# The first part of an attention and expert kernel in another order, with products of zeros on TensorE and the softmax guard on VectorE

## Chip, cores, metric

One core of one Trainium2 chip runs the whole program. The metric is the device time of one execution in microseconds (us). The engines are TensorE (PE; its weight loads are PEld), VectorE (DVE), ScalarE (ACT), GpSimd (POOL), and SyncE (SP), whose queue issues nearly all transfers. Each engine takes its instructions strictly in the order of its own row.

## The reference, cut to what matters

Three layers follow each other: sparse attention, a two-matrix layer with a PReLU, and a mixture of four experts.

```python
# attention, 2 batches x 8 heads x 768 tokens x 64: a local window and 24 block summaries
scores_l = scale * np.matmul(q, k.transpose(0, 1, 3, 2))           # kept where |i - j| < 16
scores_s = scale * np.einsum('bhsd,bhnd->bhsn', q, k_sum) + np.log(block)
a = np.exp(scores_all - np.max(scores_all, axis=-1, keepdims=True))
a = a / (np.sum(a, axis=-1, keepdims=True) + 1e-09)                # 1e-09: the guard
x = np.matmul(a, v_all)                                            # -> 1536 tokens x 512
# layer 2: 512 -> 2048 -> 512
h = x @ w_in
x = (np.maximum(h, 0.0) + alpha * np.minimum(h, 0.0)) @ w_out
# layer 3: four experts, 512 -> 1024 -> 512 each
for e in range(E):
    out += p[:, e:e + 1] * (np.maximum(x @ w1[e], 0.0) @ w2[e])
```

## The kernel before, in words

Every product that needs full precision is made of three: each operand is split into a high and a low part (h and l in the names), and high by high, high by low and low by high are added up in PSUM.

The program has a first part, ordered by hand, and a second one, which a scheduler orders. The first part holds the whole attention, a quarter of layer 2 (the first four of sixteen blocks of the inner dimension) and the preparation of the first sixteen weight pieces. The second part holds the rest of layer 2 and the experts.

The attention runs over 24 half tiles (128 tokens by four heads). A half tile goes through these steps, each with its two letters in the order: load of keys (`fa`), queries (`fb`) and values (`fc`); scores on TensorE (`sa`, line 219); masked maximum on VectorE (`sb`, line 229, eight instructions); exponentials with their row sums on ScalarE (`sc`, line 238); the guard, which adds 1e-9 to the four sums (`na`, line 245, on GpSimd); its reciprocal on VectorE (`nb`, line 248); the scaling on ScalarE (`nc`, line 257); four transposes on TensorE (`ta`, line 263); their copy on ScalarE (`tb`); the value product (`xa`, line 281); and its split into high and low (`xb` on ScalarE, `xc` on VectorE, line 298). `ka`, `kb`, `kc` load and reduce the block maxima of the keys, `va` to `vf` the block sums of the values.

A weight piece comes as 64-bit numbers, and VectorE and ScalarE turn it into two 32-bit ones: `wa` loads it, `wb` to `wh` and `wj` are seven instructions of VectorE but for `wc` (ScalarE), `wi` is the high part on ScalarE. Pieces 0 to 3 and 4 to 7 are those of `w_in` and `w_out` that the first quarter of layer 2 needs. `la` to `le` are the first product of layer 2 for 256 tokens and one piece, with its PReLU and its split; `ma` and `mb` are the second product and its copy. `pa` is the first product of the second part, drawn ahead.

`ORDER` is one string of such steps, played once from left to right: each step appends its instructions to the rows of its engines and its transfers to SP's queue. A step that has to wait holds back everything behind it on its engine, and nothing on the others. A transfer also waits for the one that used its completion lane before it.

Of the kernel before, what the change touches and what calls it, by code (L numbers as in the profile page):

```python
# [8 lines left out]
F32 = mybir.dt.float32  # L9
# [3 lines left out]
ALU = mybir.AluOpType  # L13
# [4 lines left out]
P = 128  # L18
# [15 lines left out]
G = 4  # L34
# [6 lines left out]
CH = 512  # L41
# [7 lines left out]


ORDER = (
# [34 lines left out]
)  # L86
MASK_OFF = -1.0e9 * math.sqrt(D)
EXP_LOW = float((1023 - 127 + 20) << 20)
# [4 lines left out]
def kernel(  # L93
# [15 lines left out]
    nc = tc.nc  # L109
# [4 lines left out]
    ps_2 = ctx.enter_context(tc.tile_pool(name="ps_2", bufs=3, space=PSUM))  # L114
# [4 lines left out]
    att1 = first.enter_context(tc.tile_pool(name="att1", bufs=1))  # L119
# [13 lines left out]

    ident = att1.tile([P, P], F32, name="ident")
    mask = att1.tile([P, 3, NK], F32, name="mask")
    ksum = att1.tile([P, HP, 1, NB], F32, name="ksum")

    kwb = [[att1.tile([P, NK // NB, 2, 2, NB], F32, name=f"kw{hh}{i}") for i in range(3)] for hh in range(2)]
# [3 lines left out]
    st = {"kv": 0}  # L142
# [11 lines left out]
    def half_tile(i):  # L154
        b, r = divmod(i, 2 * NAC)
        return b, r // 2, r % 2
# [51 lines left out]
    def load_vw(i):  # L208
        b, ac, hh = half_tile(i)
        st["vc", b, ac] = t = v_free.pop(0)  # L210
        nc.sync.dma_start(out=t[0:KW], in_=vw_in[b, ac])

    def a_scores(i):
        b, ac, hh = half_tile(i)
        q, kw = st.pop(("q", i)), st.pop(("kw", i))
        kw_free[hh].append(kw)
        st["s", i] = sp = ps_s.tile([P, 4, NK], F32, tag="s", name="s")
        for u in range(4):
            nc.tensor.matmul(sp[:, u], q[:, u // 2, u % 2], kw[:, :, u // 2, u % 2], start=True, stop=True)  # L219
# [22 lines left out]

    def a_guard(i):
        st["r", i] = r = att.tile([P, 4], F32, tag="r", name="r", bufs=3)
        nc.gpsimd.tensor_scalar(r, st.pop(("e", i)), 1e-9, None, op0=ALU.add)

    def a_recip(i):
        nc.vector.reciprocal(st["r", i], st["r", i])
# [290 lines left out]
    def split3(ps, terms):  # L539
        n = len(terms)  # L540
        for i, (a, c) in enumerate(terms):
            ins = nc.tensor.matmul(ps, a, c, start=(i == 0), stop=(i == n - 1))  # L542
        return ins

    def l1_product(i, c0, n):
        wh, wl = ws[0, i]
        c = slice(c0, c0 + n)
        ps = ps_1.tile([P, n], F32, tag="l1", name="l1")
        terms = []
        for k in range(KD):  # L550
            kk = slice(k * P, (k + 1) * P)
            terms += [(wh[:, kk], xh[:, k, c]), (wh[:, kk], xl[:, k, c]), (wl[:, kk], xh[:, k, c])]
        split3(ps, terms)
        gs[i, c0] = [ps]
# [288 lines left out]
    def l2_steps(u):  # L843
        n, c0, size = units[u]
        return [lambda d=d: l2a(n, d, c0, size) for d in range(KD)]
# [12 lines left out]
    load_q(2, nc.scalar)  # L858
    nc.scalar.dma_start(out=mask, in_=mask_in)
    nc.scalar.dma_start(out=ident, in_=ident_in)  # L860
    nc.gpsimd.memset(ebias, -EXP_LOW)
    nc.gpsimd.memset(vs, 0.0)
    nc.scalar.activation(early, ebias, AF.Exp)
# [6 lines left out]
    def column(f):  # L870
        return lambda u, d, *on: f(0, d, u * C0, C0, *on)

    stage = {
        "pa": lambda: l1_product(G, 0, CH),
        "ka": k_load, "kb": k_max, "kc": k_copy,
        "va": v_load, "vb": v_sum, "vc": v_rows,
        "vd": lambda b: v_mean(b, 0), "ve": lambda b: v_mean(b, 1), "vf": v_copy,
# [9 lines left out]
    with tc.manual_schedule():  # L887
        for x in ORDER.split():
            a, on = (x[2:-1], x[-1:]) if x[-1] in "vg" else (x[2:], "")
            ins = stage[x[:2]](*((int(a),) if x[0] in "fsntxw" else [int(c) for c in a]), *on)  # L890
            if x[:2] in ("ma", "wa", "le"):
                final[x[:2]] = ins
    for ins in final.values():
# [49 lines left out]
    with tc.manual_schedule(engines={mybir.EngineType.PE, mybir.EngineType.Activation}):  # L943
        left, keep, carry = [], [], []
        l2 = l2_steps(len(units) - 1)[KD // 2:]
# [7 lines left out]
        def standard(s, l2, left):  # L953
            p1, p2, p6, p5, p7, p4, p3 = e_steps(s)
            if s > NQ and not left:
                left, l2 = l2[:2], l2[2:]
            if s == NQ - 1:
                for k in range(2):
                    own_sums(k, False)
            for f in [p1] + left[:1] + [p2] + carry[:1] + [p6] + carry[1:2] + left[1:] + [p5] + carry[2:] + [p7]:  # L960
                f()
            side = e_prep(s + 1)
            carry[:] = []
            if s + 1 < NQ and (s + 1) % 2 == 0:
                side, carry[:] = side[:-3], side[-3:]
            if s in own_at:
                side = side[:3] + own_at[s] + side[3:]
            keep = l2[-1:] if s == 2 * NQ - 1 else []
            merge(l2[:len(l2) - len(keep)], side)
            return [lambda i=i, s=s: l2b(s, i) for i in range(NAC)], [p4, p3], keep  # L970
# [24 lines left out]
        for s in range(UA):  # L995
            l2, left, _ = standard(s, l2, left)
# [3 lines left out]
        for a in range(UA, UB, 2):  # L1000
# [7 lines left out]
            else:  # L1008
                n = 13 - done
# [10 lines left out]
        l2, left = [lambda i=i: l2b(UB, i) for i in range(NAC)], []  # L1020
        for s in range(UB + 1, 2 * NQ):
            l2, left, keep = standard(s, l2, left)
# [62 lines left out]
```

## Time and profile before

| | us |
|---|---|
| median of 3 runs | 833.74 |
| lowest, highest | 833.1, 835.07 |
| the profiled execution, as timed | 835.03 |
| its span, first to last instruction | 833.2 |

The profiled execution is the upper end of the three. Its span leaves out 1.83 us of its own time. The profile says of each engine when it was busy and what ended its waits. Since TensorE is busy for 98% of the span, the few places where it waits or runs at half its clock are what an edit can win; all other engines matter only where TensorE waits for them.

### The profile page before, as it was taken

How to read it: one execution, taken by the hardware profiler on the slowest of the kernel's cores; microseconds unless marked ns; L12 is line 12 of the kernel's file. 1: busy time of each engine (PE TensorE's matmuls, PEld its weight loads, DVE VectorE, ACT ScalarE, POOL GpSimd, SP SyncE). 2: the span in 40 equal slices, each digit the busy share in tenths (PEclk: the TensorE clock that was granted, in tenths of full speed). 3: DMA queues.
4: the chain of work that ended last, by engine and by line, in shares of the span. 5: the costliest groups of instructions: out<-in, count | busy, mean ns of one | idle time of the engine just before them, and what ended most of it. 6: DMA issues, size and time to landing. Idle time of an engine off the chain costs nothing.

```text
span 833.2 us, 14458 instructions
## 1 busy us (share of the span) xinstructions
PE 814.2 (98%) x5000; PEld 746.2 (90%) x5000; DVE 612.6 (74%) x1284; ACT 424.9 (51%) x1048; POOL 307.5 (37%) x302
## 2 busy tenths in 40 slices
PE   4899999999999999999999999999999999999998
PEld 3689999888888888988989989989999999999997
DVE  7998667999993446587687687687677677768765
ACT  5999995543442333353454454464455454455430
POOL 1110100000013100386886886789153354354330
PEclk9799999999999999999999999999999999999999
DMA  9999413333222100367867867869766856767622
GB/s 340 298 276 303 145 45 102 102 101 101 95 84 76 51 1 0 102 205 263 284 214 267 282 212 271 276 233 324 263 226 202 266 187 220 246 209 238 201 72 76
DMA packets 97496, 155.37 MB, mean 186 GB/s; under 512 B 9872, under 2 KB 48272, under 8 KB 97424
## 3 DMA queue, kind: packets, MB, share of 16 engines
q1 hardware_dynamic: 96704, 153.92, 56.8%
q8 instruction: 39, 0.64, 0.3%
q10 hardware_dynamic: 720, 0.55, 0.2%
q14 instruction: 33, 0.27, 0.1%
HBM read 106.71 MB, written 47.71 MB: 185 GB/s over the span
## 4 chain that ended last, share of the span: by engine, by line
PE 91%; DMA 3%; DVE 3%; ACT 2%; issue 0%; SPq 0%; POOL 0%; ACTq 0%
PE l L542 48%; PE cb L662 16%; PE l2q L784 13%; PE cd L662 8%; PE ca L662 4%; PE s L219 1%; PE xps L281 1%; DMA kw<-in_kw 1%; DMA vcat<-in_vw 1%; PE pt L263 1%; DMA acc<-in_kt 1%; ACT sm L238 1%; DMA bl<-dt 0%; DVE xel L617 0%; DVE sm L229 0%; DVE ksum L169 0%
## 5 line engine op out<-in xcount | busy, mean ns | idle before, releaser
L391 POOL TENSOR_TENSOR w0l<-ra,w0h 128x256 fp32r<-128x256 f32 (+1 forms) x32 | 37.6, 1176 | 237.1 <-ACT w0h L390 237.1
L831 DVE SCALAR_TENSOR_TENSOR acc<-l,prob_sb,acc 128x512 f32<-128x512 f32 x101 | 74.2, 746 | 26.0 <-PE l L542 25.8
L795 DVE SCALAR_TENSOR_TENSOR acc<-l2q,prob_sb,acc 128x256 f32<-128x256 f32 x156 | 71.2, 478 | 27.3 <-PE l2q L784 25.4
L542 PE MATMUL l<-xh,w0h 128*128 128x512 f32 (+1 forms) x240 | 84.5, 352 | 0.0
L542 PE MATMUL l<-gh,w1h 128*128 128x512 f32 (+1 forms) x240 | 83.3, 350 | 0.0
L542 PE MATMUL l<-xl,w0h 128*128 128x512 f32 (+1 forms) x240 | 83.1, 346 | 0.0
L542 PE MATMUL l<-xh,w0l 128*128 128x512 f32 (+1 forms) x240 | 83.1, 346 | 0.0
L542 PE MATMUL l<-gh,w1l 128*128 128x512 f32 (+1 forms) x240 | 83.0, 347 | 0.0
L542 PE MATMUL l<-gl,w1h 128*128 128x512 f32 (+1 forms) x240 | 81.4, 347 | 0.0
L542 PE MATMUL l<-w1h,gl 128*128 128x512 f32 x192 | 75.0, 391 | 0.0
L542 PE MATMUL l<-w1l,gh 128*128 128x512 f32 x192 | 75.0, 391 | 0.0
L542 PE MATMUL l<-w1h,gh 128*128 128x512 f32 x192 | 74.7, 389 | 0.0
L567 DVE SCALAR_TENSOR_TENSOR l<-m,beta,l 128x512 f32<-128x512 f32 (+1 forms) x60 | 38.6, 644 | 23.8 <-ACT m L561 23.7
L685 ACT ACTIVATE u<-cb 128x384 f32<-128x384 f32 x64 | 31.3, 489 | 47.5 <-PE cb L662 47.5
L561 ACT ACTIVATE m<-l 128x512 f32<-128x512 f32 (+1 forms) x60 | 30.6, 513 | 48.2 <-PE l L542 48.1
L542 PEld LDWEIGHTS l<-xh,w0h 128*128 128x128 f32 x240 | 45.4, 189 | 5.9
L542 PEld LDWEIGHTS l<-gh,w1h 128*128 128x128 f32 x240 | 45.4, 189 | 5.7
L542 PEld LDWEIGHTS l<-gh,w1l 128*128 128x128 f32 x240 | 45.4, 189 | 5.6
L542 PEld LDWEIGHTS l<-xl,w0h 128*128 128x128 f32 x240 | 45.4, 189 | 5.6
L542 PEld LDWEIGHTS l<-gl,w1h 128*128 128x128 f32 x240 | 45.4, 189 | 5.5
L542 PEld LDWEIGHTS l<-xh,w0l 128*128 128x128 f32 x240 | 45.3, 189 | 5.6
L391 POOL TENSOR_TENSOR w1l<-rb,w1h 128x512 fp32r<-128x512 f32 x32 | 43.9, 1391 | 11.9 <-ACT w1h L390 11.9
(167 smaller groups left out, 2534.3 us busy)
## 6 DMA issues: line engine op xcount, KB each, us to landing
raw<-in_wa SPq DMA_DIRECT2D x32, 512.0 KB, 3.9
rb<-in_wb SPq DMA_DIRECT2D x16, 512.0 KB, 4.8
ra<-in_wb SPq DMA_DIRECT2D x32, 256.0 KB, 3.6
dt<-xh SPq DMA_DIRECT2D x28, 256.0 KB, 2.4
dt<-xl SPq DMA_DIRECT2D x28, 256.0 KB, 3.3
bh<-dt SPq DMA_DIRECT2D x28, 256.0 KB, 3.7
bl<-dt SPq DMA_DIRECT2D x28, 256.0 KB, 3.7
q<-in_qh SPq DMA_DIRECT2D x23, 256.0 KB, 5.8
```

The costliest lines, as they stand in the source:

```text
L219: nc.tensor.matmul(sp[:, u], q[:, u // 2, u % 2], kw[:, :, u // 2, u % 2], start=True, stop=True)
L238: nc.scalar.activation(sm[:, u], sm[:, u], AF.Exp, bias=mx[:, u:u + 1], scale=-1.0, accum_out=sume[:, u:u + 1],)
L263: nc.tensor.transpose(pt[0:NK, u], pp[:, u], ident)
L391: nc.gpsimd.tensor_tensor(lo, src, hi.bitcast(F32), op=ALU.subtract)
L542: ins = nc.tensor.matmul(ps, a, c, start=(i == 0), stop=(i == n - 1))
L561: nc.scalar.activation(m, gs[i, c0][0], AF.Relu, scale=-1.0)
L567: nc.vector.scalar_tensor_tensor(ps, m, beta[:, i:i + 1], ps, op0=ALU.mult, op1=ALU.add)
L662: nc.tensor.matmul(ps, l, r, start=(first and i == 0), stop=(i == len(terms) - 1), skip_group_check=True)
L685: nc.scalar.activation(v[name], ps, AF.Copy)
L784: nc.tensor.matmul(ps, l, r, start=(first and j == 0), stop=(j == len(terms) - 1), skip_group_check=True)
L795: nc.vector.scalar_tensor_tensor(dst, ps, pe, dst, op0=ALU.mult, op1=ALU.add)
L831: added = nc.vector.scalar_tensor_tensor(acc2[:, t], ps, pe, acc2[:, t], op0=ALU.mult, op1=ALU.add)
```

## The change

Three edits, all in the first part. `ORDER` is a new string: the same steps, in another sequence. A new step `zz` followed by a number n issues n products of a 128 x 128 tile of zeros with itself into a PSUM tile that nobody reads; nine such steps, 39 products in all, stand among the first TensorE steps, the last just ahead of the first value product. The guard `na` moves from GpSimd to VectorE. A clearing of the tile of zeros is added on GpSimd. Of the order only the first line stands here.

```diff
 ORDER = (
-    "wa5 wd5 wb5 we5 ka01 wc5 kb01 ka00 fa2 kb00 kc00 sa2 wf5 wa3 wg5 fa0 wh5 wb3 wd3 fb0 wi5 ka03 sa0 "
...
+    "wa5 wd5 ka01 wb5 wc5 we5 ka00 kb01 wf5 wa3 kb00 wg5 kc00 wd3 fa2 wh5 wi5 wb3 fa0 we3 fb0 wj5 wa2 "
+    "zz15 sa2 zz1 wc3 fb4 fa4 sb2 ka02 wf3 wb2 sa0 zz5 sc2 na2 wd2 wc2 sb0 sc0 wg3 fb1 nb2 sa4 zz2 na0 "
...
+    zero = att1.tile([P, P], F32, name="zero")
...
+    zps = ps_2.tile([P, P], F32, tag="l2", name="zps")
+
+    def spin(n):
+        for _ in range(n):
+            nc.tensor.matmul(zps, zero, zero, start=True, stop=True)
...
     def a_guard(i):
         st["r", i] = r = att.tile([P, 4], F32, tag="r", name="r", bufs=3)
-        nc.gpsimd.tensor_scalar(r, st.pop(("e", i)), 1e-9, None, op0=ALU.add)
+        nc.vector.tensor_scalar(r, st.pop(("e", i)), 1e-9, None, op0=ALU.add)
...
+    nc.gpsimd.memset(zero, 0.0)
...
-        "pa": lambda: l1_product(G, 0, CH),
+        "zz": spin, "pa": lambda: l1_product(G, 0, CH),
```

On TensorE, at the start of the program, stood scores (`s`), transposes (`pt`) and nothing else:

```order
L219 MATMUL s<-kw_97,q 128x120 x4
L219 MATMUL s<-kw_98,q 128x120 x4
L219 MATMUL s<-kw_99,q 128x120 x4
L263 MATMUL pt<-ident,sm 120x128 x4
L219 MATMUL s<-kw_100,q 128x120 x4
```

On TensorE, at the same place, `zps` is the tile that the products of zeros write:

```order
L218 MATMUL zps<-zero 128x128 x15
L226 MATMUL s<-kw_98,q 128x120 x4
L218 MATMUL zps<-zero 128x128
L226 MATMUL s<-kw_99,q 128x120 x4
L218 MATMUL zps<-zero 128x128 x5
L226 MATMUL s<-kw_100,q 128x120 x4
L218 MATMUL zps<-zero 128x128 x2
L270 MATMUL pt<-ident,sm 120x128 x4
```

Each group of zeros stands ahead of a step that TensorE reached early before.

On VectorE, ahead of the first masked maximum (`ISA sm,mx`), stood two block maxima together and the preparation of one and a bit weight pieces:

```order
L169 TENSOR_REDUCE ksum<-acc 128x24 x2
L174 COPY kw_97<-ksum 128x96
L338 TENSOR_SCALAR e<-e 128x512
L342 SCALAR_TENSOR_TENSOR e<-raw,e 128x512
L348 TENSOR_TENSOR t<-t,e 128x512
L314 TENSOR_SCALAR e<-raw 128x512
L327 TENSOR_SCALAR t<-raw 128x512
L229 ISA sm,mx<-s,mask 128x120
```

On VectorE, at the same place, now:

```order
L170 TENSOR_REDUCE ksum<-acc 128x24
L345 TENSOR_SCALAR e<-e 128x512
L170 TENSOR_REDUCE ksum<-acc 128x24
L349 SCALAR_TENSOR_TENSOR e<-raw,e 128x512
L175 COPY kw_98<-ksum 128x96
L334 TENSOR_SCALAR t<-raw 128x512
L355 TENSOR_TENSOR t<-t,e 128x512
L321 TENSOR_SCALAR e<-raw 128x512
L341 SCALAR_TENSOR_TENSOR t<-raw,t 128x512
L367 TENSOR_TENSOR w1l<-t,w1h 128x512
L236 ISA sm,mx<-s,mask 128x120
```

One weight instruction moved between the two block maxima, and two more (lines 341 and 367, before at 334 and 360) moved ahead of the maximum.

On VectorE, behind that maximum, stood weights and a block maximum, then the next masked maximum:

```order
L229 ISA mx 128x1
L338 TENSOR_SCALAR e<-e 128x512
L334 SCALAR_TENSOR_TENSOR t<-raw,t 128x512
L169 TENSOR_REDUCE ksum<-acc 128x24
L229 ISA sm,mx<-s,mask 128x120
```

On VectorE, at the same place, with the first guard (`r<-sume`):

```order
L236 ISA mx 128x1
L345 TENSOR_SCALAR e<-e 128x512
L321 TENSOR_SCALAR e<-raw 128x512
L252 TENSOR_SCALAR r<-sume 128x4
L334 TENSOR_SCALAR t<-raw 128x512
```

The guard now stands two instructions behind the maximum whose exponentials it has to wait for.

## Rows read from the trace of the kernel before

**Rows 1.** The page: the span, and the chain that ended last, by engine.

```profile
span 833.2 us, 14458 instructions
...
PE 91%; DMA 3%; DVE 3%; ACT 2%; issue 0%; SPq 0%; POOL 0%; ACTq 0%
```

**Rows 2.** Busy time by stage: stretch, length, PE, PEld, DVE, ACT, POOL, clock, DMA share, GB/s.

```profile
4.90:69.30 64.40, 53.68 (x476) 47.39 (x476) 61.16 (x226) 56.73 (x209) 7.93 (x23) 0.92 1.01 314
69.30:149.50 80.20, 80.20 (x796) 78.22 (x793) 57.49 (x194) 66.00 (x231) 4.21 (x14) 1.00 0.44 133
...
149.50:833.20 683.70, 680.31 (x3734) 620.55 (x3732) 493.99 (x866) 300.69 (x608) 294.63 (x259) 1.00 0.55 181
...
150.00:160.00 10.00, 10.00 (x46) 8.28 (x45) 9.35 (x19) 6.18 (x13) 0.00 (x0) 1.00 0.40 113
```

**Rows 3.** Timeline: start, length, engine, line, operation; idle before and what ended it.

```profile
67.80 1.48 DVE L360 TENSOR_TENSOR w1l<-t,w1h 128x512 fp32r<-128x512 f32 x2
...
69.33 0.39 PE L542 MATMUL l<-gh,w1h 128*128 128x256 f32 x1
...
149.53 0.40 PE L542 MATMUL l<-xh,w0h 128*128 128x512 f32 x1
```

**Rows 4.** Timeline of VectorE from its first instruction to the end of the first maximum.

```profile
4.90 0.43 DVE L327 TENSOR_SCALAR t<-raw 128x512 uint32<-128x512 uint32 x1 [4.90 <-DMA raw<-in_wa]
...
6.27 0.95 DVE L169 TENSOR_REDUCE ksum<-acc 128x24 f32<-128x768 f32 x1
7.63 0.95 DVE L169 TENSOR_REDUCE ksum<-acc 128x24 f32<-128x768 f32 x1 [0.41 <-DMA acc<-in_kt]
...
11.27 0.27 DVE L229 CUSTOM_DVE_ANT_0 sm<-s,mask 128x120 f32<-128x120 f32 x1
...
12.08 0.42 DVE L338 TENSOR_SCALAR e<-e 128x512 uint32<-128x512 f32 x1
```

**Rows 5.** Timeline of ScalarE: first and last part of the first exponentials.

```profile
11.86 0.38 ACT L238 ACTIVATE sm<-sm,mx 128x120 f32<-128x120 f32 x1
...
13.28 0.19 ACT L238 ACTIVATION_READ_ACCUMULATOR sm<-sm,mx 128x1 f32 x1
```

**Rows 6.** Timeline of VectorE: its two longest waits between 8 and 69 us.

```profile
39.95 0.42 DVE L298 TENSOR_TENSOR xl<-xps,xh 128x256 fp32r<-128x256 f32 x1 [0.82 <-ACT xh L152]
...
45.12 0.42 DVE L298 TENSOR_TENSOR xl<-xps,xh 128x256 fp32r<-128x256 f32 x1 [0.54 <-ACT xh L152]
```

**Rows 7.** Timeline of TensorE: four score products at either clock (x8 counts two passes each).

```profile
8.88 2.06 PE L219 MATMUL s<-kw,q 128*128 128x120 f32 x8 [8.88 <-DVE kw L174]
...
41.51 1.15 PE L219 MATMUL s<-kw,q 128*128 128x120 f32 x8
```

**Rows 8.** Busy time and granted clock (third from the end) in short stretches.

```profile
22.00:24.00 2.00, 1.80 (x9) 1.26 (x8) 2.00 (x9) 2.00 (x9) 0.22 (x1) 1.00 1.04 398
...
30.00:32.00 2.00, 1.53 (x18) 1.09 (x17) 1.86 (x4) 1.86 (x6) 1.94 (x3) 0.50 1.08 335
38.00:40.00 2.00, 2.00 (x21) 1.88 (x21) 1.18 (x5) 0.96 (x3) 0.00 (x0) 0.53 1.05 264
```

**Rows 9.** The guard on GpSimd, its reciprocal on VectorE until 69.3 us, and one reciprocal's neighbours.

```profile
L245 POOL TENSOR_SCALAR r<-sume x24: 222/222/687, 13.6 to 117.7; 128x4 f32<-128x4 f32 x24
...
L248 DVE RECIPROCAL r<-r 128x4 f32<-128x4 f32 x12 | 2.1, 172 | 0.2
...
24.41 0.17 DVE L248 RECIPROCAL r<-r 128x4 f32<-128x4 f32 x1
24.50 0.67 DVE L360 TENSOR_TENSOR w0l<-t,w0h 128x512 fp32r<-128x512 f32 x1
```

**Rows 10.** Timeline of VectorE and GpSimd around one long guard.

```profile
29.79 0.69 DVE L342 SCALAR_TENSOR_TENSOR e<-raw,e 128x512 uint32<-128x512 uint32 x1
30.59 0.18 DVE L248 RECIPROCAL r<-r 128x4 f32<-128x4 f32 x1
...
29.92 0.64 POOL L245 TENSOR_SCALAR r<-sume 128x4 f32<-128x4 f32 x1 [4.05 <-ACT sm L238]
```

More of the change, by code (lines that the diff above doesn't have):

```diff
@@ L889 @@
             a, on = (x[2:-1], x[-1:]) if x[-1] in "vg" else (x[2:], "")
-            ins = stage[x[:2]](*((int(a),) if x[0] in "fsntxw" else [int(c) for c in a]), *on)
+            ins = stage[x[:2]](*((int(a),) if x[0] in "fsntxwz" else [int(c) for c in a]), *on)
             if x[:2] in ("ma", "wa", "le"):
```

65 rows, old and new, of the table ORDER are left out of this document.

## The prediction, made before the changed kernel ran

> **What bounds the kernel now.** I read the page first: the chain that ended last is 91% TensorE [rows 1]. Then the busy time by stage, where the reader should compare TensorE's column with the length of the stretch [rows 2]. From 69.30 to 149.50 us TensorE is busy for all 80.20 us at full clock, and in the 683.70 us behind that it lacks only 3.4 us, at the program's end and in places that this change does not touch. So the time is: the moment from which TensorE never waits again, plus a fixed amount of work. Everything that the change can win or lose in its own part lies ahead of that moment.
>
> Which moment is it? The timeline gives it [rows 3]. VectorE works on the last two low parts of the first `w_out` pieces from 67.80 until 69.28, and TensorE starts the first second product of layer 2 at 69.33, 0.05 us later. The first product of the second part behind the pre-drawn one starts at 149.53, 80.20 us later, with no wait between. TensorE's own row cannot be shortened from there: the new order has the same products behind this point, with 80.20 us of work. So **what sets the end is when VectorE gets through its row up to those low parts.** VectorE starts at 4.90, when the first weights land [rows 4], and is busy for 61.16 of the next 64.40 us [rows 2]. Its row is nearly full: 3.24 us are all that any order can take out of it as long as the same instructions stand ahead of that point. They do: counted in the two orders, the set of VectorE's instructions up to the low part of piece 4 is the same, plus twelve guards.
>
> ScalarE is the second engine at its limit, with 56.73 us busy of these 64.40, and GpSimd (7.93 us) and TensorE (53.68 us) are not.
>
> **The guard.** Twelve guards come ahead of the point, as twelve reciprocals do [rows 9]. I take a reciprocal of the same 128 x 4 tile as the price of a guard on VectorE: it lasts 0.17 us, but the next instruction starts 0.09 us after it (24.41 to 24.50). So 12 x 0.09 = **+1.1 us**; bounds 0, if each falls into a wait that VectorE has anyway, and 12 x 0.17 = 2.1, if none overlaps.
>
> What goes away on GpSimd was off the path (0.22 us each, one up to 0.69) [rows 9]. The row shows one effect on VectorE: beside the long guard at 29.92 the next instruction of VectorE starts 0.80 us after the one at 29.79, which lasts 0.69, so there is a hole of 0.11 us [rows 10]. I take 0.2 us for two such places: **-0.2**; bounds 0 and 12 x 0.11 = -1.3. The Trainium skill (SBUF — State Buffer, section "Who interferes with whom") says that VectorE and GpSimd share a pair of ports which one instruction holds alone while the other waits in full. By that rule each guard could hold VectorE for as long as it lasts, and taking twelve away would give back 12 x 0.22 = 2.6 us. The trace agrees that somebody waits, but it is the guard that gets longer (0.64 instead of 0.22 us), and VectorE loses 0.11. What the rule would make of the sum stands among the rivals.
>
> **The guard's place.** On GpSimd a guard that waits for its exponentials holds up nobody. On VectorE it holds up the whole row. At the first guard: before, the first maximum starts at 11.27 and ends 0.81 us later [rows 4]; the exponentials run from 11.86 to 13.47 [rows 5]. In the new row two more instructions of 512 columns come ahead of the maximum, each about 0.7 us (two low parts take 1.48) [rows 3], and the wait of 0.41 us for the keys' transfer is filled by a weight instruction that was moved into it [rows 4]. So the maximum starts at 11.27 + 1.4 - 0.4 = 12.3, and VectorE reaches the guard after 0.81 for the maximum and two instructions of 0.34 to 0.43 each, at about 13.9. The exponentials start 0.3 to 0.6 us behind the maximum's start and take 1.61: they end between 14.2 and 14.5. The guard waits 0.3 to 0.6 us: **+0.45**. Behind it wait the next weight step and the next maximum, and behind that one ScalarE. The wait for the keys gives **-0.4**. Bounds for all guards together: 0, and as the rival below has it.
>
> **The products of zeros.** A score step of four products takes 2.06 us at 8.88, where TensorE begins, and 1.15 at 41.51 [rows 7]. The granted clock is 1.00 at 22 to 24 us, 0.50 at 30 to 32 and 0.53 at 38 to 40 [rows 8]: full is 2.4 GHz, half is 1.2, and the first step has the time of half. One product of zeros of nearly the same size thus costs 0.3 to 0.5 us, all 39 together 11 to 20 us. TensorE has 10.7 us without work in 4.90 to 69.30 [rows 2] and nothing to do before 8.88 us [rows 7], so they cover waits; the first fifteen take 4 to 8 us from about 1 us on and are done when the first score's keys are there. I take 0 for what they hold up; bounds 0 and one group of five at half clock, 2.5 us, which only counts if it reaches VectorE.
>
> What they can win is the longer steps at half clock. VectorE's two longest waits behind the start, 0.82 us at 39.95 and 0.54 at 45.12 [rows 6], are for high parts of value products that TensorE made at or just behind half clock. If the clock stays up, I take both as gone: **-0.8 - 0.5**; bounds 0 and all of VectorE's 3.24 us of idle time.
>
> **The rest of the order.** Behind 149.5 us VectorE is busy for 9.35 of 10 us [rows 2], and all 24 guards, 24 x 0.09 = 2.2 us, are in its way by then. It had 80.20 - 57.49 = 22.7 us free between 69.30 and 149.50, so I take 0; bounds 0 and +1 us, should a weight piece be late for TensorE there.
>
> **The sum.** +1.1 - 0.2 + 0.45 - 0.4 - 0.8 - 0.5 = about -0.4 us. The profiled execution took 835.03, its span plus 1.83, and stands 1.29 us above the median of the runs; the sum is a difference within one execution, so I put it on the median: 833.74 - 0.4 = **833.3 us**.
>
> **Rivals.**
> 1. *VectorE never waits.* The new order takes out all 3.24 us of idle time and keeps the guards: -3.24 + 1.1 = -2.1, 831.6 us. For it: two of the waits hang on TensorE's half clock. Against it: part of the idle time is holes of a tenth that any order has, and the first guard adds a new wait.
> 2. *The ports' rule.* The guards on GpSimd cost VectorE their whole 0.22 us: -2.6 in place of -0.2, so -2.8, 830.9 us. Against it: [rows 10] show 0.11 us at the longest guard.
> 3. *The guard as a stopper (slower).* Not one but five of the twelve guards make VectorE wait 0.45 us for exponentials, since ScalarE too is nearly full and runs behind. Then +1.1 - 0.2 - 0.4 - 0.8 + 5 x 0.45 = +1.95: 835.7 us. It decides from the fifth such wait on; with fewer it stays within the forecast. For it: the first one comes out of the sum above.
> 4. *The clock falls all the same.* No zeros stand behind the first value product, and at 30 to 40 us TensorE's own work is thin: the two waits of rows 6 stay, +1.3 on the forecast, 834.6 us. For it: before, the clock went to half with TensorE busy for 1.53 of 2 us.
>
> **How the numbers follow.** A measurement of this kernel can tell about 0.2%, 1.7 us, from no change: below 832.1 is faster, above 835.4 slower. The forecast has 0.45, rival 4 0.10: together 0.55 for no difference. Rival 1 has 0.17 and rival 2 0.06: 0.23 for faster. Rival 3 has 0.22. The range goes down to 831.5, which takes in rival 1, and up to 835.8, which takes in rival 3; rival 2 and a longer row of stopping guards are left out.
>
> **What would show it.** In the changed kernel the low parts of the fourth `w_out` piece should end at about 69 us, TensorE's first second product should follow at once, and the second part should start at about 149. The granted clock should be full from the first few us to at least 30; a half-clock stretch behind 30 is rival 4. Waits of VectorE at the guard's line, with ScalarE's exponentials as what ended them, are rival 3 if their sum passes 2 us. If TensorE does not wait for VectorE at that product, or waits in the second part, the argument as a whole is wrong.

## The result and the profile after

| | us |
|---|---|
| changed kernel, median of 6 runs | 838.31 (837.80 to 838.71) |
| kernel before, beside it, median of 6 | 833.42 (832.90 to 835.07) |
| ratio, 95% interval | 1.0056 (1.0046 to 1.0066) |
| profiled execution, its span | 838.47, 836.7 |

The change makes the kernel 4.7 us slower (0.0056 x 833.4). The forecast was 833.3 us with a range up to 835.8. The ratios are given as they were recorded, with their intervals; a ratio need not be the quotient of the two medians beside it.

The profile on which the prediction rests is of an execution at the upper end of the kernel before (835.03). The kernel before was therefore profiled once more (832.98 us, "the second trace of before"), and the comparison goes by that one. First the page of the changed kernel, its span and the chain that ended last. It answers to [rows 1]: VectorE's share rises from 3 to 4%, TensorE's falls to 90%.

```profile
span 836.7 us, 14605 instructions
...
PE 90%; DVE 4%; DMA 2%; ACT 2%; issue 0%; POOL 0%; ACTq 0%; POOLq 0%
```

Busy time by stage as in [rows 2]: from VectorE's start to the hand-over (TensorE's first second product of layer 2, just behind VectorE's last two low parts), from there to the second part, and the second part. Changed kernel:

```profile
5.88:71.32 65.44, 55.01 (x532) 49.57 (x531) 61.87 (x238) 56.69 (x208) 5.86 (x11) 0.92 0.92 302
71.32:153.49 82.17, 80.75 (x796) 78.35 (x794) 55.79 (x200) 66.78 (x233) 1.63 (x2) 1.00 0.37 123
153.49:836.70 683.21, 679.98 (x3734) 620.59 (x3732) 496.78 (x871) 300.74 (x608) 294.61 (x259) 1.00 0.54 182
```

The second trace of before, the same three stages:

```profile
4.86:67.83 62.97, 53.72 (x477) 47.87 (x477) 60.92 (x226) 56.55 (x209) 7.96 (x23) 0.92 0.99 324
67.83:148.03 80.20, 80.20 (x797) 78.25 (x794) 57.64 (x194) 65.92 (x230) 4.07 (x14) 1.00 0.42 130
148.03:831.20 683.17, 679.96 (x3734) 620.52 (x3732) 493.27 (x866) 300.55 (x608) 294.37 (x259) 1.00 0.54 181
```

The second part lasts 683.2 us in both. All of the loss lies ahead of it, 153.49 - 148.03 = 5.46 us between these two executions, in four pieces. They say where the time lies, not yet what caused it:
- VectorE starts 5.88 - 4.86 = 1.02 us later.
- VectorE waits 65.44 - 61.87 = 3.57 us in the first stage, in place of 62.97 - 60.92 = 2.05: +1.52 (against the first trace of before, with 3.24, only +0.33).
- VectorE is busy for 0.95 us more, with twelve guards more.
- TensorE, which was to be busy without a gap in the second stage, waits 82.17 - 80.75 = 1.42 us there, and is busy for 0.55 us more (the cause of these 0.55 is open).

The hand-over that [rows 3] show, now:

```profile
69.90 1.29 DVE L367 TENSOR_TENSOR w1l<-t,w1h 128x512 fp32r<-128x512 f32 x2
...
71.32 0.36 PE L549 MATMUL l<-gh,w1h 128*128 128x256 f32 x1
...
153.49 0.40 PE L549 MATMUL l<-xh,w0h 128*128 128x512 f32 x1
```

The two ends lie close together again, but TensorE does not wait for VectorE there, in either kernel: it comes to the product straight from other work. In the trace that the prediction rests on, its last wait ahead of 149.53 ends at 61.16, and was for a load of values:

```profile
61.16 1.15 PE L281 MATMUL xps<-ptb,vcat 120*64 120x64 f32 x32 [0.80 <-DMA vcat<-in_vw]
...
68.71 0.69 PE L281 MATMUL xps<-ptb,vcat 120*64 120x64 f32 x16
69.33 0.39 PE L542 MATMUL l<-gh,w1h 128*128 128x256 f32 x1
```

Nor is VectorE the fullest engine ahead of the hand-over. From 16 us until then, in the second trace of before, ScalarE (the fourth busy time) is busy for 51.28 of 51.83 us and VectorE (the third) for 50.34:

```profile
16.00:67.83 51.83, 47.60 (x453) 42.52 (x453) 50.34 (x194) 51.28 (x190) 6.74 (x19) 0.90 0.98 312
```

In the changed kernel ScalarE lacks 3.20 us in the same stretch, in place of 0.55:

```profile
16.00:71.32 55.32, 48.90 (x500) 43.62 (x499) 52.39 (x207) 52.12 (x196) 4.32 (x8) 0.97 0.92 296
```

VectorE's waits until 80 us, from the view of waits (what waited, for what; us in total, times, longest):

```profile
DVE t L334 <- DMA raw<-in_wa: 5.9, 1, 5.9
DVE r L252 <- ACT sm L245: 5.1, 4, 2.4
DVE e L321 <- DMA raw<-in_wa: 1.6, 2, 1.1
```

`r` at line 252 is the guard: it waits 5.1 us for ScalarE's exponentials, in four times (0.40, 0.75, 1.58 and 2.41 us). The last one lies behind the hand-over and shows how such a wait travels. In the timeline, VectorE, ScalarE and TensorE:

```profile
77.14 0.17 DVE L252 TENSOR_SCALAR r<-sume 128x4 f32<-128x4 f32 x1 [2.41 <-ACT sm L245]
...
78.50 0.25 DVE L236 CUSTOM_DVE_ANT_0 sm<-s,mask 128x120 f32<-128x120 f32 x1
...
75.48 0.39 ACT L245 ACTIVATE sm<-sm,mx 128x120 f32<-128x120 f32 x1
...
76.91 0.20 ACT L245 ACTIVATION_READ_ACCUMULATOR sm<-sm,mx 128x1 f32 x1
...
79.42 1.15 PE L226 MATMUL s<-kw,q 128*128 128x120 f32 x8 [1.26 <-DVE mx L236]
```

ScalarE comes to these exponentials only at 75.48, and the guard starts as they end. A maximum queued behind the guard on VectorE starts at 78.50, a score tile becomes free late, and TensorE loses 1.26 us at a score product.

The granted clock did what it was to do for a part only: full (2.4 GHz) from 5.4 to 8.8 us, half from 8.8 to 15.6, full, and half once more from 29.3 to 32.7 (third number from the end). Ahead of the first fall TensorE had ended its first zeros at 6.69 and had nothing to do until 10.70:

```profile
5.40:8.80 3.40, 1.28 (x12) 1.09 (x10) 2.79 (x6) 0.72 (x1) 0.00 (x0) 1.00 1.04 388
8.80:15.60 6.80, 4.90 (x23) 4.93 (x24) 6.28 (x23) 3.45 (x11) 1.54 (x3) 0.50 0.92 311
...
29.30:32.70 3.40, 3.40 (x19) 3.40 (x18) 3.40 (x14) 3.29 (x14) 0.00 (x0) 0.50 1.06 258
```

### The profile page after: what moved, and what is told of

Its sections match the earlier page's. It is cut to its first block, busy times and chain, and to the rows that moved or that the text cites. A ratio compares the mean times of both kernels' runs of the same rounds, so it can differ in the third digit from the quotient of the medians.

```text
span 836.7 us, 14605 instructions
## 1 busy us (share of the span) xinstructions
PE 820.6 (98%) x5078; PEld 753.4 (90%) x5078; DVE 614.4 (73%) x1308; ACT 425.7 (51%) x1048; POOL 303.0 (36%) x279
## 4 chain that ended last, share of the span: by engine, by line
PE 90%; DVE 4%; DMA 2%; ACT 2%; issue 0%; POOL 0%; ACTq 0%; POOLq 0%
PE l L549 47%; PE cb L669 16%; PE l2q L791 13%; PE cd L669 8%; PE ca L669 4%; DMA raw<-in_wa 1%; DVE sm L236 1%; PE xps L288 1%; ACT sm L245 1%; DMA ident<-in_ident 1%; PE s L226 1%; PE pt L270 1%; ACT sm L264 1%; DVE ksum L170 1%; DVE vs L181 0%; DVE l L574 0%
```

## Experiments: the three edits apart

Three theories. A: the guards, placed early, stop VectorE's row. B: the new order loses by itself. C: the zeros cost. Four kernels take the edits apart.

**Order and zeros, guard back on GpSimd** (e1)

```diff
-        nc.vector.tensor_scalar(r, st.pop(("e", i)), 1e-9, None, op0=ALU.add)
+        nc.gpsimd.tensor_scalar(r, st.pop(("e", i)), 1e-9, None, op0=ALU.add)
```

> The changed kernel with one edit undone: the guard is back on GpSimd; new order and zeros stay. Theory A (the guard stops VectorE's row): VectorE's waits at the guard until 80 us (0.40, 0.75, 1.58 and 2.41 us in the changed kernel) shrink to what the reciprocals behind them wait, and 1.1 us of guards leave the row: 834 to 835.5 us. Theory B (the new order itself, with its weight transfer ahead of the keys, is worse): 837 to 838.5 us. Theory C (the zeros hold up scores): 837 to 838.5 us too.

Measured 835.68 us, ratio 1.0022 (1.0012 to 1.0031), just above theory A's range; the second part starts at 150.55.

**Order and guard, no zeros** (e2): the nine `zz` steps leave `ORDER`.

> The changed kernel without the 39 products of zeros; new order and guard on VectorE stay. Theory A and theory B: within 0.7 us of the changed kernel's 838.3, or slower if the zeros had kept the clock up (up to 839.5). Theory C: the score that waited behind five products of zeros at half clock comes 1.6 us earlier, 836.5 to 837.5 us.

Measured 837.96 us, ratio 1.0043 (1.0029 to 1.0056); the guards wait 6.2 us in four times until 80 us. VectorE starts at 4.89, 1 us earlier than in the changed kernel, and the second part starts at 153.49 all the same.

**The order alone** (e3): both edits undone.

> The new order alone, on the kernel before: guard on GpSimd, no zeros. Theory A: within 1 us of before, 832.5 to 834.5 us. Theory B: most of the 4.9 us are here, 836.5 to 838.5 us. Theory C: as A.

Measured 835.26 us, ratio 1.0011 (0.9999 to 1.0023), between the two ranges; the second part starts at 150.32.

**The guard alone, in the old order** (e4)

> The kernel before with the guard on VectorE, in the old order, where it now stands just ahead of its reciprocal or a few steps before it. Theory A: slower by the guards' 1.1 us and by waits for exponentials, 835.5 to 838 us. Theory B: at most the guards' own time, 833.4 to 834.5 us.

Measured 833.52 us, ratio 0.9995 (0.9987 to 1.0003); the second part starts at 149.04. The waits that theory A expected in this order did not come.

What follows: the chain order alone, with zeros, with guard is 1.0011, 1.0022, 1.0056, that is +0.9, +0.9 and +2.8 us. Without the zeros the guard's step is from 1.0011 to 1.0043, +2.7. Only the guard's step is clear of the intervals, by either path; the steps of the order and, within it, of the zeros are not. Nor do the steps simply add up: without zeros the changed kernel's second part starts no earlier (e2). The guard costs 2.8 us in the new order and nothing that can be measured in the old one. So what costs is not the instruction by itself but where it stands. In the old order it waits for ScalarE once until 80 us, and behind the hand-over:

```profile
DVE r L245 <- ACT sm L238: 0.9, 1, 0.9
```

## Experiments: the guard's place and its price

**Each guard directly ahead of its reciprocal** (e5), zeros kept; one of the 24 places:

```diff
-  ... sa0 zz5 sc2 na2 wd2 wc2 sb0 sc0 wg3 fb1 nb2 sa4 ...
+  ... sa0 zz5 sc2 wd2 wc2 sb0 sc0 wg3 fb1 na2 nb2 sa4 ...
```

> The changed kernel with each of the 24 guards moved in VectorE's row to directly ahead of its reciprocal; the same instructions, zeros kept. Theory A (a guard placed early stops VectorE's row while ScalarE ends the exponentials): the waits at the guard's line fall from 5.1 us in four to under 1 us until 80 us, the second part starts at about 151 instead of 153.5 us, and the time falls from 838.3 to about 836 us, which is the time with the guard on GpSimd (835.7) plus what twelve instructions cost (0 to 1.1). Rival (a guard on VectorE costs by its own length and by what it does to the engine, wherever it stands): no change, 838.3.

Measured 836.58 us, ratio 1.0039 (1.0026 to 1.0052); the second part starts at 151.41, 2.08 us earlier than in the changed kernel. No wait at the guard's line is left until 80 us, and TensorE no longer waits behind the hand-over. That is 1.4 us (0.0017 x 833.4) back by moving instructions alone, though the two intervals overlap. The kernel with the guard on GpSimd (e1) is another 1.4 us faster. The timeline of VectorE shows what is left:

```profile
26.48 0.16 DVE L253 TENSOR_SCALAR r<-sume 128x4 f32<-128x4 f32 x1
26.68 0.18 DVE L256 RECIPROCAL r<-r 128x4 f32<-128x4 f32 x1
26.77 0.92 DVE L182 TENSOR_REDUCE vs<-acc 128x24 f32<-128x768 f32 x1
```

The reciprocal reads what the guard writes and starts 0.20 us behind it; the reduction, which reads neither, starts 0.09 us behind the reciprocal.

**The guard twice, in the old order** (e8): the price by itself.

```diff
         nc.vector.tensor_scalar(r, st.pop(("e", i)), 1e-9, None, op0=ALU.add)
+        nc.vector.tensor_scalar(r, r, 0.0, None, op0=ALU.add)
```

> The old order with the guard on VectorE, and behind each guard a second one that adds 0 to the same four numbers, so that only the price of 24 more such instructions changes, not what is waited for; no zeros. If the price is 0.09 us as worked out, the twelve ahead of the fourth output piece add 1.1 us to the old order with one guard (833.5): 834.6, second part at 150.1. If they fall into holes of VectorE's row: 833.5, second part at 149.0. At their full 0.17 us: 835.6.

Measured 835.22 us, ratio 1.0021 (1.0011 to 1.0030); the second part starts at 149.60. Timeline of VectorE with one guard (e4):

```profile
13.95 0.16 DVE L245 TENSOR_SCALAR r<-sume 128x4 f32<-128x4 f32 x1
14.02 0.27 DVE L229 CUSTOM_DVE_ANT_0 sm<-s,mask 128x120 f32<-128x120 f32 x1
```

and with two:

```profile
13.98 0.16 DVE L252 TENSOR_SCALAR r<-sume 128x4 f32<-128x4 f32 x1
14.18 0.17 DVE L253 TENSOR_SCALAR r<-r 128x4 f32<-128x4 f32 x1
14.25 0.28 DVE L236 CUSTOM_DVE_ANT_0 sm<-s,mask 128x120 f32<-128x120 f32 x1
```

The second guards cost 0.0026 x 833.4 = 2.2 us; by these rows 12 x 0.20 = 2.4, more than the 0.17 of my upper bound. (The second parts of the two traces differ by only 0.56 us: that of e4 is of its slowest execution, 834.16.) A guard with other work behind it takes 0.07 us of VectorE's row; one whose result the next instruction reads takes 0.20. By these rows the twelve guards of e5 take 2.4 us that e1 does not have. Measured are 1.4; a wait of 0.5 us for a guard on GpSimd, which e1 has, is gone in e5.

**Each guard one step of VectorE ahead of its reciprocal** (e11), so that other work lies between the two:

> The changed kernel with each guard one step of VectorE ahead of its reciprocal (a weight instruction, a maximum, a reduction or a split lies between the two), in place of directly ahead of it. In the trace of the kernel with the guards directly ahead, the reciprocal starts 0.20 us behind its guard, since it reads what the guard writes; between independent instructions of that size 0.09 us. Theory: 12 x 0.11 = 1.3 us go from VectorE's row up to the fourth output piece, and no guard waits as long as in the changed kernel: time 835.3 to 836. Rival (one step earlier already stops the row): guard waits of over 1 us in sum until 80 us, 836.6 or above.

Measured 836.46 us, ratio 1.0041 (1.0026 to 1.0056); the second part starts at 151.34. The time is that of e5, so the expected 1.3 us did not come: a guard waits again, 1.1 us in one time. With these intervals (1.2 us either way) the run does not settle whether one step ahead is better than none.

## Experiments: the zeros

**Zeros in the old order** (e6), guard on GpSimd: `zz15` ahead of the first scores, 24 more behind the same early scores and transposes.

> The old order with the guard on GpSimd and 39 products of zeros at the matching places (fifteen ahead of the first scores, the rest behind the same early scores and transposes). Theory Z1 (the early zeros make the first weight piece land late): VectorE starts at 5.8 instead of 4.9 us, and the second part starts up to 0.9 us later than in the kernel before, 150.0 to 150.4; time 834.0 to 834.4. Theory Z2 (as predicted: the zeros hold up nothing and keep the clock up): VectorE starts at 4.9 and loses its waits of 0.82 and 0.54 us; second part at 148.5, time 832.5.

Measured 834.90 us, ratio 1.0019 (1.0011 to 1.0027). The profiled execution was the quickest of twelve (833.84, second part at 148.74), so it was profiled again:

> The old order with the guard on GpSimd and 39 zeros once more, for a second trace: the first was of the quickest of its twelve executions (833.8, median 834.9). If an execution near 834.9 differs by the landing of the first weight piece, VectorE starts near 6.5 us instead of 5.5; if it differs by waits in the row, VectorE's idle time up to the fourth output piece is near 3 us instead of 1.9.

This one took 835.68 us: VectorE starts at 5.80, waits 1.0 us for a weight piece and 1.2 us for high parts, and the second part starts at 150.70. What varies is mostly the row's waits (1.9 and 3.7 us up to the hand-over), less the first landing (5.52 and 5.80).

**Zeros only once the first weights are there** (e7), new order, guard on GpSimd: VectorE clears the tile of zeros behind its first weight instruction.

```diff
-    nc.gpsimd.memset(zero, 0.0)
...
+        "zm": lambda u: nc.vector.memset(zero, 0.0),
```

> The new order with the guard on GpSimd and all 39 zeros, but the tile of zeros is cleared by VectorE behind its first weight instruction, so that no product of zeros can start before about 5.4 us. Theory Z1 (zeros that run while the first loads are under way delay them): VectorE starts at 4.9 us as in the kernel without zeros, and the time falls from 835.7 to about 835 us. Rival (the late landing has to do with the program's size or its instructions, not with when the zeros run): VectorE starts at 5.8, time 835.7 or above, since the first scores now wait behind the zeros.

Measured 834.96 us, ratio 1.0024 (1.0009 to 1.0039), with the widest spread of all (833.36 to 839.90). In the trace, of the slowest execution, the first product of zeros came at 6.12, and VectorE still started at 5.50. So it is not the running zeros that delay the landing.

**Only the 16 later zeros, old order** (e12), none ahead of the first transposes.

> The old order with the guard on GpSimd and only the 16 later zeros, behind the first transposes until the first value product; none while the first loads are under way or ahead of the first scores. Theory (the early zeros cost by the late first landing, the later ones keep the clock up): VectorE starts at 4.9 us, the clock stays full from about 16 to 40 us, time 832.3 to 833. Rival (zeros win nothing in an ordinary execution of the old order): 833.5 to 834; if VectorE starts at 5.5 or later all the same, it is the products' presence in TensorE's row and not their place.

Measured 834.78 us, ratio 1.0013 (1.0004 to 1.0021). VectorE starts at 5.50, though the first product of zeros comes at 17.82. The clock stays full, and it wins nothing. Busy time from 26 to 38 us with the 16 zeros, then in the second trace of before (the fifth number is VectorE's, 0.57 against 1.00 is the clock):

```profile
26.00:38.00 12.00, 9.20 (x101) 7.45 (x100) 11.72 (x38) 11.91 (x41) 3.09 (x5) 1.00 1.05 271
```

```profile
26.00:38.00 12.00, 9.67 (x80) 8.84 (x80) 11.68 (x43) 11.50 (x39) 2.56 (x4) 0.57 0.95 260
```

VectorE is busy for 11.7 of 12 us either way: in this stretch TensorE keeps up with it at half clock too.

**One zero** (e13) and **all 39 at the end of the first part** (e14), old order, guard on GpSimd:

> The old order with the guard on GpSimd and one single product of zeros, behind the first transposes. In six kernels with 16 or 39 of them VectorE started at 5.50 to 5.94 us, in five with none at 4.86 to 5.01, also where the first product of zeros came long behind the landing. Theory N (it grows with the number of instructions added to TensorE's row): VectorE starts at about 4.9 to 5.0, time 833.4. Rival (any product of zeros at all does it): VectorE starts at 5.5 or later, time 834.2 to 834.8.

> The old order with the guard on GpSimd and all 39 products of zeros at the end of the first part, ahead of the first product of the second part, where TensorE never waits. The time must grow by what they last at full clock, 39 x 0.2 = about 8 us; what is asked is the start. Theory N (number of instructions in TensorE's row): VectorE starts at 5.5 us or later. Rival (only instructions near the row's start count): VectorE starts at 4.9 to 5.0.

One zero: 833.24 us, ratio 0.9992 (0.9980 to 1.0004). All at the end, one execution: 844.06 us; the products last from 141.49 on for 8.97 us. What was asked is the start. First instruction of VectorE with one zero:

```profile
5.09 0.43 DVE L334 TENSOR_SCALAR t<-raw 128x512 uint32<-128x512 uint32 x1 [5.09 <-DMA raw<-in_wa]
```

and with the 39 at the end, where no zero runs for the first 141 us:

```profile
5.58 0.43 DVE L334 TENSOR_SCALAR t<-raw 128x512 uint32<-128x512 uint32 x1 [5.58 <-DMA raw<-in_wa]
```

So the start goes with how many products are added, not with when they run. The page's list of DMA queues has a counterpart. With one zero it shows, on the queue that brings instructions (packets, MB, share):

```profile
q8 instruction: 39, 0.64, 0.3%
```

and with 39 at the end:

```profile
q8 instruction: 40, 0.66, 0.3%
```

All 19 traces of this case fall into two groups: nine with 39 packets, in which VectorE starts at 4.85 to 5.09 us, and ten with 40, in which it starts at 5.50 to 6.20. The Trainium skill (Runtime: NRT & Kernel Launch, section "Instruction fetch mechanics") says that instructions are fetched in blocks of 16 KiB and that a further block is mostly hidden. The packets agree (0.66 MB / 40 = 16.5 KB); "hidden" does not, if the block is the cause. That the block is the cause is not shown: the two go together in 19 of 19 traces, but no packet of that queue lies in the first 10 us of any of them, and all the added instructions were products of zeros.

**A second trace of the kernel before** (e9):

> The kernel before, unchanged, for a second trace: the one on which the prediction rests is of an execution 1.3 us above the median. Theory V (that execution had waits which an ordinary one has not): in an execution near 833.5 the two waits of VectorE of 0.82 and 0.54 us for high parts of value products at half clock are absent or shorter, and the second part starts at about 148.2. Rival (they belong to the kernel): both waits are there again within 0.2 us, and what differs lies elsewhere.

832.98 us, one execution. Of the two waits of [rows 6], the one of 0.82 us is gone; the one of 0.54 is there:

```profile
39.08 0.42 DVE L298 TENSOR_TENSOR xl<-xps,xh 128x256 fp32r<-128x256 f32 x1
...
44.25 0.42 DVE L298 TENSOR_TENSOR xl<-xps,xh 128x256 fp32r<-128x256 f32 x1 [0.54 <-ACT xh L152]
```

VectorE waits 2.05 us in this stage, not 3.24 as in [rows 2], and the second part starts at 148.03. Theory V is half right: 0.82 us of what the zeros were to win belonged to one execution.

## Experiments: the order's own loss

**The keys' load ahead of the second weight piece's** (e15), order alone otherwise:

```diff
-  ... kb01 wf5 wa3 kb00 wg5 kc00 wd3 fa2 wh5 ...
+  ... kb01 wf5 fa2 wa3 kb00 wg5 kc00 wd3 wh5 ...
```

> The new order with the guard on GpSimd and no zeros, as in the run of the order alone (835.3), but with the second keys' load issued ahead of the second weight piece's load, as in the kernel before. Theory B (the new order's own loss begins with the keys that land at 9.4 instead of 7.9 us, so that TensorE's first scores start at 9.7 instead of 8.9): scores start at 8.9 or earlier, VectorE's two waits of 0.43 and 0.46 us at 16.6 and 20.3 go, time 834.0 to 834.4. Rival (the loss sits in the row's later waits): 835 to 835.6.

Measured 833.74 us, ratio 0.9998 (0.9987 to 1.0010): the order's loss is gone, though the two intervals overlap; the second part starts at 148.52 in place of 150.32. Timeline of the order alone (e3): SyncE's issue of the keys, and TensorE's first scores.

```profile
4.88 2.06 SPq L202 DMA_DIRECT2D kw<-in_kw  x2
...
9.73 2.67 PE L226 MATMUL s<-kw,q 128*128 128x120 f32 x11 [9.73 <-DVE t L334]
```

With the keys first (e15), and the wait that it brings:

```profile
2.10 0.59 SPq L202 DMA_DIRECT2D kw<-in_kw  x1
...
9.44 1.78 PEld L226 LDWEIGHTS s<-kw,q 128*128 128x128 f32 x8 [9.44 <-DVE kw L175]
9.44 2.06 PE L226 MATMUL s<-kw,q 128*128 128x120 f32 x8 [9.44 <-DMA prob_sb<-in_probs]
10.71 0.43 DVE L334 TENSOR_SCALAR t<-raw 128x512 uint32<-128x512 uint32 x1 [1.32 <-DMA raw<-in_wa]
```

SyncE issues four loads at once; the fifth goes out when the first has landed (4.88, with VectorE's start at 4.89). In the new order the keys were that fifth load. The expectation had its size right and its path only in part: the scores start 0.29 us earlier, not 0.8 (their weight loads wait for VectorE's copy of the block maxima, line 175; the releaser in the row of the products is not what scores read), and of the two waits that were to go, the one of 0.46 us at the reciprocal stays. The weight piece is now the late one (1.32 us), yet the row loses less: up to the hand-over VectorE waits 2.59 us in place of 3.43, and its 225 instructions keep it busy for 60.82 us in place of 61.52. Why the same instructions take less, and which of the later steps gains the rest, isn't shown.

**The same load put back in the changed kernel** (e16), zeros and early guards kept:

> The changed kernel, zeros and early guards and all, with the one transfer put back: the second keys' load ahead of the second weight piece's load. If the causes add up, it gains what it gained without the other two edits, 1.5 us: 838.3 to 836.8. If the early guards and zeros hide it (VectorE waits for exponentials anyway): 838 or above.

Measured 838.54 us, ratio 1.0052 (1.0039 to 1.0066): nothing gained that can be measured; the second part starts at 153.29, and VectorE at 6.20, later than in any other trace. VectorE's waits until 80 us:

```profile
DVE r L253 <- ACT sm L246: 5.5, 5, 2.4
```

Waits at guards take the place of the one that was removed: five now, 5.5 us. The losses of single edits don't add up: with the early guards in place, neither the zeros (e2) nor the keys (e16) give anything back.

**All three undone** (e17): keys first, guards directly ahead of the reciprocals, no zeros; the new order and the guard on VectorE stay.

> The new order with the keys' load put back, each guard on VectorE directly ahead of its reciprocal, and no zeros: the three causes undone, the new order and the guard on VectorE kept. If these three are the whole loss but for the price of a guard that its reciprocal waits for (12 x 0.2 = up to 2.4 us at the most, 0.9 by the run with the guards directly ahead against the one with the guard on GpSimd): 833.7 to 834.8. If something of the order remains: 835.5 or above.

Measured 835.00 us, ratio 1.0013 (1.0004 to 1.0021); VectorE starts at 4.85. The time lies between the two ranges. What is left, 1.1 us, is of the size of the price of the dependent pairs: against e15, which differs by the guard alone, 0.0015 x 833.4 = 1.25 us, and e5 against e1 gave 1.4. The intervals (some 0.8 us either way) would hide another loss of that size. No kernel here beats the one before; one zero, the keys first, and the guard alone in the old order are level with it.

## Why the prediction was wrong

The forecast missed by 5.1 us: -0.4 against +4.7. By the point values of the chain order, zeros, guard, the terms of the guard missed by 2.8 - 1.35 = 1.45, that of the keys by 1.3, and those of the zeros and the clock by 2.2. But only the guard's loss is clear of the intervals, and with the guards in their early places undoing the zeros or the keys alone gives nothing back that can be measured.

- **What bounds the kernel: the second part right, the moment wrong.** The second part is a constant (683.17 and 683.21 us). The moment is not the hand-over: TensorE does not wait for VectorE at that product in any trace here, which the prediction itself had named as a sign against the argument as a whole. Two ends 0.05 us apart were read as a wait. And ScalarE is fuller than VectorE from 16 us on (51.28 and 50.34 of 51.83 us), so VectorE's row alone was not the thing to count. Which of the two rows sets the end in the kernel before was not tested; that a guard costs nothing measurable on VectorE in the old order (e4) fits a fuller ScalarE, and with the second guards of e8, where the time rises, VectorE is the fuller one (52.83 and 52.02 of 53.40 us). "TensorE never waits again" failed too: the changed kernel lost 1.42 us behind the hand-over, 1.26 of them because a guard stopped VectorE there. I had looked for guards only ahead of it.
- **The guard's place, +0.45: mis-sized, and the loss that the runs show best.** The edit costs 2.8 us in this order, with its own instructions in it. I worked out the first guard in the row and let it stand for the other eleven. That one doesn't wait at all: a weight piece lands 0.52 us late just ahead of it, and the exponentials are done by then. Three others wait 2.7 us ahead of the hand-over, and a fourth 2.41 behind it. The mechanism was written down as the third rival, with the right chain behind it, and its sign, waits of over 2 us in sum, came true; but it was priced from that first guard at 0.45 each, and the four took 0.40 to 2.41. The order showed each guard's distance from its maximum, and ScalarE had 56.73 us of work in 64.40 [rows 2]: both spoke for a long wait at any guard that stands a few instructions behind its maximum.
- **The keys, -0.4: wrong in sign.** I counted the weight instruction that fills VectorE's wait, and not the transfers that are moved with it. The second weight piece's load went ahead of the keys' in SyncE's queue, the keys became the fifth load, and the order alone costs 0.9 us (1.0011, an interval that takes in no loss), all of it given back by one swap (0.9998).
- **The zeros hold up nothing, 0: wrong by 1 to 1.6 us in the old order** (1.0013 and 1.0019). A first landing that comes 0.4 to 1.35 us later in every program with 16 or more of them was not in view, where the products themselves were. That it makes up the whole cost is not shown.
- **The clock, -0.8 - 0.5: wrong.** 0.82 was a wait of one execution. And VectorE is as busy at half clock as at full in that stretch (11.68 and 11.72 of 12 us). The fourth rival's observation, that the clock falls again at 30 us, came true (29.3 to 32.7), and it was at half from 8.8 to 15.6 already; no run gives a sign that this cost anything.
- **The guard's price, +1.1: right in size by the rows alone.** They give 12 x 0.07 = 0.84 us where other work stands behind it, and 0.20 each where the reciprocal does, which [rows 9] could not show. The time of the old order shows none of the 0.84 (e4).
- **GpSimd's guards, -0.2, and the ports' rule: not the gain of the rule.** The Trainium skill's rule (SBUF — State Buffer, "Who interferes with whom") would, priced as in the prediction, have given 2.6 - 0.84 = 1.8 us back in the old order. That price takes every instruction of VectorE as one that shares the ports, while that section of the Trainium skill limits the lock to some of them. The guard alone measured -0.4 (interval -1.1 to +0.25): less than the 1.8, while a smaller gain can't be told from the price of the guards.
- **The second part, 0: right.**
- **The base.** The sum was put on the median, which was right. But its terms were taken from a trace 1.3 us slower, so a wait of that execution was entered as something to win.

## What to carry over

An instruction that waits for another engine is not costed by its length when it moves to the bound engine's row: work out its wait for every copy of it, not for the first, and remember that it may stop the row behind the point you watch as well. When an order moves loads, number them in their queue; the one that becomes the first to wait for a landing is the edit. Two ends that lie close together are not yet a wait: look whether the engine was idle between them. And profile the kernel before twice before you enter a wait as a gain.

## What was not expected of the hardware

- A pair of small instructions of VectorE (128 x 4) of which the second reads the first costs 0.20 us from start to start, against 0.07 to 0.09 for independent ones.
- The first load (512 KB) lands at 4.85 to 5.09 us with 39 packets of instructions in the program and at 5.50 to 6.20 with 40, wherever the added products stand. Why is open.
- Keeping TensorE's clock at 2.4 GHz showed no gain where VectorE and ScalarE were full: with the clock at 0.57 or at 1.00 over 12 us, VectorE was busy for 11.68 and 11.72 us.
